# GpSimd shares in unpacking the first two weights and forms w_in's sums, with a new order of work up to the first products

## The chip, the cores and the metric

The kernel runs on one core of a Trainium2 chip. Its engines work side by side, each through its own list of instructions in order, and wait for each other by semaphores: TensorE (PE in the profile, its weight loads PEld), VectorE (DVE), ScalarE (ACT), GpSimd (POOL) and SyncE (SP), which issues the transfers. The metric is the device time of one execution in microseconds; lower is better.

## The reference

Attention within chunks of 64 rows, then two MLPs on 2304 tokens of width 512:

```python
q_c = q.reshape(B, H, nc, 64, D)            # B 4, H 8, 9 chunks, D 64; k, v alike
scores = scale * np.matmul(q_c, k_c.transpose(0, 1, 2, 4, 3))
attn = softmax(scores)                      # max taken off, sum + 1e-9
x = heads_side_by_side(np.matmul(attn, v_c))        # 2304 x 512
h = x @ w_in                                # 512 x 2048
g = np.maximum(h, 0.0) + alpha * np.minimum(h, 0.0)
x = g @ w_out                               # 2048 x 512
out = ((x @ w_a) * (x @ w_b)) @ w_out2      # 512 x 1536 twice, 1536 x 512
```

The weights come in as 64-bit floats; the kernel reads each as two 32-bit words and unpacks them itself.

## The kernel before

A float32 product is made of three matmuls on rounded parts: every operand is split into a high part `hi` (a rounded copy, made by ACT in `to_hi`, L88) and a low part `lo` (the rest, made by DVE in `to_lo`, L93), and `three` (L390) multiplies high by high, high by low and low by high.

A weight passes through three stages. `w_load` (L113) brings a raw tile of 128 x 1024 words in by a transfer on SP. `unpack_ops` (L127) makes 512 floats per row of it: one step widens the upper word by a scale of 2^-112 into the tile `wx`; two 16-bit steps form `wz`, its lower half from the lower word's upper bits and its upper half from the sign bit; a last DVE step (L159) shifts `wx` left by three and puts `wz` in. With `act_first` 2, ACT does the widening (L140) and the lower half of `wz` (L145), DVE the sign (L156) and the combining. Then `w_parts` takes the result and `to_hi` and `to_lo` split it. The units of weights are, in order, i0, i1, i2, o0, i3, o1, i4, o2 and so on, where i is a tile of w_in and o one of w_out; raw tiles 0, 1, 2 lie in three staging buffers that later loads reuse.

The tokens go in blocks of 512, 256, 512, 512 and 512. The first block's attention is four units of 128 tokens, written out by hand in one string, `order1` (L1198): each word is a letter and a number, and the string is the order in which instructions enter the engines' lists. F n: n filler transposes on PE. k, q: transposes of k and q. S: scores. M: maximum and subtraction. X: exponential. N: one step of four of the softmax's division. P: transpose of the probabilities. O: product with v. H, L: high and low part of the attention result x. U i: one step of three of unpacking weight i. C, D: high and low part of a weight (ACT, DVE). A2, A4: the first projection (weight i0) over the first and the second 256 tokens of the block. B, G: the activation's parts. After the string the loop over 16 tiles j of w_in runs (L1310): `s1` projects with i j, `s2` accumulates with o j two tiles behind, and `prelu_unpacking` (L433) makes the activation and unpacks two further weights for each j of the first block.

PSUM tiles for the early attention are taken in turn from two pools of four banks (`att_bank`, L289); a bank is free when its last reader is done.

In blocks 1 and 2 `keep_sum` (L167) adds the two parts of each w_in tile up to the whole value again, and `keep_out` (L174) writes it to DRAM (`wd`), 16 tiles, to be read back for blocks 3 and 4. POOL is used for the identity matrix and constants alone.

Of the kernel before, what the change touches and what calls it, by code (L numbers as in the profile page):

```python
# [8 lines left out]
F32 = mybir.dt.float32  # L9
F32R = mybir.dt.float32r  # L10
I32 = mybir.dt.int32
U16 = mybir.dt.uint16
AF = mybir.ActivationFunctionType
ALU = mybir.AluOpType
# [4 lines left out]
def chunk_attention_prelu_mlp_bilinear_mlp(  # L19
# [17 lines left out]
    nc = tc.nc  # L37
# [38 lines left out]
    def bank(nm="ps"):  # L76
        return ps_p.tile([P, DM], F32, tag="ps", name=nm)
# [6 lines left out]
    def wtile(name, dt=F32R):  # L84
        return wp.tile([P, DM], dt, tag="w", name=name)

    def to_hi(hi, lo, src):
        nc.scalar.activation(out=hi, in_=src, func=AF.Copy)  # L88

    def to_lo(hi, lo, src):  # L90
        if lo is None:
            return
        nc.vector.tensor_tensor(out=lo, in0=src, in1=hi.bitcast(F32), op=ALU.subtract)  # L93

    def split(*a):
        to_hi(*a)
        to_lo(*a)
# [13 lines left out]
    W, raws, xs, slots = {}, {}, {}, {}  # L111
# [15 lines left out]
    def unpack_ops(i, act_first=False):  # L127

        raw = raws.pop(i)
        hw = raw.rearrange("p (f t) -> p f t", t=2)[:, :, 1]
        xs[i] = x = wtile("wx", I32)
        z = wtile("wz", I32)
        z2 = z.bitcast(U16).rearrange("p (f t) -> p f t", t=2)
        h2 = raw.bitcast(U16).rearrange("p (f t) -> p f t", t=4)

        def widen():
            return nc.scalar.activation(out=x.bitcast(F32), in_=hw.bitcast(F32), func=AF.Copy, scale=2.0 ** -112)  # L140

        if act_first == 2:

            widen()
            yield nc.scalar.activation(  # L145
                out=z2[:, :, 0], in_=h2[:, :, 1], func=AF.Copy, scale=2.0 ** -13, bias=2.0 ** -14 - 0.5
            )
        else:
            if act_first:
                yield widen()  # L150
            yield nc.vector.tensor_scalar(
                out=z2[:, :, 0], in0=h2[:, :, 1], scalar1=13, scalar2=None, op0=ALU.logical_shift_right
            )
            if not act_first:
                yield widen()
        yield nc.vector.tensor_scalar(  # L156
            out=z2[:, :, 1], in0=h2[:, :, 3], scalar1=1 << 15, scalar2=None, op0=ALU.bitwise_and
        )
        yield nc.vector.scalar_tensor_tensor(  # L159
            out=x, in0=x, scalar=3, in1=z, op0=ALU.logical_shift_left, op1=ALU.bitwise_or  # L160
        )

    wd = [dr.tile([P, DM], F32, name=f"wd{j}") for j in range(J1)]

    whole = []

    def keep_sum(j):  # L167

        hi, lo = W["i", j]
        x = wtile("wi", F32)  # L170
        nc.vector.tensor_tensor(out=x, in0=hi.bitcast(F32), in1=lo.bitcast(F32), op=ALU.add)
        whole.append((j, x))

    def keep_out(n):  # L174
# [209 lines left out]
    def xtiles(nm):  # L384
        return (
            xp.tile([P, KD, NB], F32R, tag="xh", name=nm + "h"),
            xp.tile([P, KD, NB], F32R, tag="xl", name=nm + "l"),
        )

    def three(ps, w, x, i, n_i):  # L390
        (wh, wl), (xh, xl) = w, x
        for a, b, first in ((wh, xh, True), (wh, xl, False), (wl, xh, False)):
            nc.tensor.matmul(  # L393
                out=ps, lhsT=a, rhs=b, start=(i == 0 and first), stop=(i == n_i - 1 and a is wl)
            )

    def proj(w, x, n, ps=None, lo=0):
        ps = ps or bank("psh")
        for kk in range(KD):
            f = slice(kk * P, (kk + 1) * P)  # L400
            three(ps[:, lo:n], (w[0][:, f], w[1][:, f]), (x[0][:, kk, lo:n], x[1][:, kk, lo:n]), kk, KD)
        return ps
# [147 lines left out]
    parts = {}  # L550
# [588 lines left out]
    with tc.manual_schedule():  # L1139
# [13 lines left out]
        x = xtiles("x")  # L1153
# [17 lines left out]
        chains, parts, h0, g0 = {}, {}, [], []  # L1171

        def chained(key, chain, u):
            if (key, u) not in chains:
                chains[key, u] = chain(u)
            next(chains[key, u])
# [11 lines left out]
            "H": lambda u: each(to_hi, parts["x", u]),  # L1188
            "L": lambda u: each(to_lo, parts["x", u]),
            "W": w_dma,  # L1190
            "U": lambda i: chained("U", lambda i: unpack_ops(i, 2), i),
            "B": lambda i: nc.scalar.activation(out=beta_sb, in_=alpha_sb, func=AF.Copy, scale=-1.0, bias=1.0),
            "G": lambda i: chained("G", lambda i: prelu_parts(0, h0[0], g0, True), i),
            "C": lambda i: (parts.update({("w", i): w_parts(i)}), to_hi(*parts["w", i])),
            "D": lambda i: to_lo(*parts["w", i]),
            "A": lambda u: h0.append(proj(W["i", 0], x, u * P, *h0, lo=len(h0) * n0 // 2 * P)),
        }
        order1 = (  # L1198
# [3 lines left out]
        )  # L1202
        for t in order1.split():
            early[t[0]](int(t[1:]))
# [74 lines left out]
        for b, (t0, n) in enumerate(blocks[:bx]):  # L1279
# [66 lines left out]
            x = nxt  # L1346
# [215 lines left out]
        for p, j in seq:  # L1562
# [8 lines left out]
            if not left[j] and j + 2 < J2:  # L1571
# [5 lines left out]
                i = units.index(("b", j + 2)) + 1  # L1577
# [89 lines left out]
```

## Time and profile before

| | |
|---|---|
| time, median of 3 runs | 848.49 us (848.29 to 848.98) |
| span of the profiled execution | 845.1 us |
| PE busy | 833.5 us, 99% |
| DVE busy | 647.7 us, 77% |
| ACT busy | 420.2 us, 50% |
| POOL busy | 0.7 us, 6 instructions |

The span is that of one profiled execution, from its first to its last instruction; that execution's own time outside the profiler isn't given, so the span stands beside the median of the runs. A busy time is a union over instructions, so neighbours that overlap count once; an instruction's duration is longer than the distance to the next start on its engine. What an engine is worth is read from the stretch: which wait ends last there.

### The profile page before, as it was taken

How to read it: one execution, taken by the hardware profiler on the slowest of the kernel's cores; microseconds unless marked ns; L12 is line 12 of the kernel's file. 1: busy time of each engine (PE TensorE's matmuls, PEld its weight loads, DVE VectorE, ACT ScalarE, POOL GpSimd, SP SyncE). 2: the span in 40 equal slices, each digit the busy share in tenths (PEclk: the TensorE clock that was granted, in tenths of full speed). 3: DMA queues.
4: the chain of work that ended last, by engine and by line, in shares of the span. 5: the costliest groups of instructions: out<-in, count | busy, mean ns of one | idle time of the engine just before them, and what ended most of it. 6: DMA issues, size and time to landing. Idle time of an engine off the chain costs nothing.

```text
span 845.1 us, 14464 instructions
## 1 busy us (share of the span) xinstructions
PE 833.5 (99%) x5429; PEld 714.1 (84%) x5429; DVE 647.7 (77%) x1236; ACT 420.2 (50%) x794; POOL 0.7 (0%) x6
## 2 busy tenths in 40 slices
PE   7999999999999999999999999999999999999998
PEld 6788889988787788888888888888888888889998
DVE  5899955656778877777969888898898858848781
ACT  5998955566656553445643223323333236533440
POOL 0000000000000000000000000000000000000000
PEclk9999999999999999999999999999999999999999
DMA  9994759989963412053801554544454158825511
GB/s 214 284 287 163 200 130 222 233 206 223 231 181 100 150 50 100 26 188 136 299 26 57 187 170 149 168 177 148 155 206 144 75 198 303 282 64 176 152 60 52
DMA packets 171655, 138.86 MB, mean 164 GB/s; under 512 B 101825, under 2 KB 138177, under 8 KB 171585
## 3 DMA queue, kind: packets, MB, share of 16 engines
q1 hardware_dynamic: 171584, 137.93, 55.6%
q8 instruction: 43, 0.70, 0.4%
q14 instruction: 28, 0.22, 0.1%
HBM read 82.32 MB, written 46.40 MB: 152 GB/s over the span
## 4 chain that ended last, share of the span: by engine, by line
PE 90%; DVE 4%; ACT 3%; DMA 2%; issue 1%; SPq 0%; DVEq 0%; ACTq 0%
PE acc L393 27%; PE psh L393 11%; PE psA L615 8%; PE psD L615 8%; PE psB L615 8%; PE psr L393 4%; PE psE L615 4%; PE psD L759 3%; PE psB L759 3%; PE psA L759 3%; PE psD L1365 3%; PE psB L1365 3%; PE psA L1365 2%; PE psE L759 2%; PE psE L1365 1%; PE psSO L315 1%
## 5 line engine op out<-in xcount | busy, mean ns | idle before, releaser
L159 DVE SCALAR_TENSOR_TENSOR wx<-wx,wz 128x512 int32<-128x512 int32 x68 | 46.9, 689 | 14.3 <-ACT wx L140 10.8
L88 ACT ACTIVATE gh<-pos 128x512 fp32r<-128x512 f32 (+1 forms) x56 | 31.8, 567 | 38.8 <-DVE pos L415 32.3
L649 ACT ACTIVATE p<-psA 128x512 f32<-128x512 f32 x24 | 14.4, 598 | 71.7 <-PE psA L615 71.7
L93 DVE TENSOR_TENSOR gl<-pos,gh 128x512 fp32r<-128x512 f32 (+1 forms) x56 | 34.4, 615 | 20.2 <-ACT gh L88 19.1
L645 DVE TENSOR_TENSOR t<-p,psB 128x512 f32<-128x512 f32 x48 | 32.9, 685 | 21.4 <-PE psB L615 17.2
L415 DVE SCALAR_TENSOR_TENSOR pos<-neg,nalpha_sb,pos 128x256 f32<-128x256 f32 (+1 forms) x32 | 19.7, 617 | 28.9 <-ACT pos L413 28.6
L655 ACT ACTIVATE p<-psD 128x512 f32<-128x512 f32 x24 | 14.4, 599 | 50.9 <-PE psD L615 42.4
L411 ACT ACTIVATE neg<-psh 128x512 f32<-128x512 f32 (+1 forms) x48 | 24.7, 515 | 12.6 <-PE psh L393 12.6
L140 ACT ACTIVATE wx<-raw 128x512 f32<-128x512 f32 x48 | 30.2, 661 | 0.0
L683 ACT ACTIVATE b_sb<-psr 128x256 f32<-128x256 f32 x12 | 4.6, 382 | 51.6 <-PE psr L393 51.6
L393 PE MATMUL psr<-xrh,Tl 128*128 128x256 f32 x96 | 27.2, 283 | 0.0
L393 PE MATMUL psr<-xrl,Th 128*128 128x256 f32 x96 | 27.2, 283 | 0.0
L393 PE MATMUL psr<-xrh,Th 128*128 128x256 f32 x96 | 27.1, 282 | 0.0
L1376 DVE SCALAR_TENSOR_TENSOR pos<-neg,beta_sb,psA 128x512 f32<-128x512 f32 x8 | 6.0, 748 | 25.9 <-ACT neg L1372 25.9
L266 ACT ACTIVATE kqd<-kq 128x1024 uint16<-128x1024 uint16 x24 | 24.1, 1046 | 2.6 <-DMA kq<-in_k_dram 2.2
L156 DVE TENSOR_SCALAR wz<-raw 128x512 uint16<-128x512 uint16 x48 | 21.4, 453 | 0.0
L1372 ACT ACTIVATE neg<-p 128x512 f32<-128x512 f32 x24 | 15.2, 633 | 8.8 <-DVE p L1405 8.0
L393 PEld LDWEIGHTS psr<-xrl,Th 128*128 128x128 f32 x96 | 18.4, 192 | 0.4
L393 PEld LDWEIGHTS psr<-xrh,Th 128*128 128x128 f32 x96 | 18.4, 192 | 0.4
L1376 DVE SCALAR_TENSOR_TENSOR p<-neg,beta_sb,p 128x512 f32<-128x512 f32 x24 | 18.0, 749 | 0.8
L393 PEld LDWEIGHTS psr<-xrh,Tl 128*128 128x128 f32 x96 | 18.4, 192 | 0.0
L645 DVE TENSOR_TENSOR p<-t,p 128x512 f32<-128x512 f32 x24 | 16.6, 692 | 1.0
(949 smaller groups left out, 3009.3 us busy)
## 6 DMA issues: line engine op xcount, KB each, us to landing
raw<-in_moe_w_out_dram SPq DMA_DIRECT2D x17, 512.0 KB, 4.1
raw<-in_moe_w_a_dram SPq DMA_DIRECT2D x12, 512.0 KB, 5.1
raw<-in_moe_w_b_dram SPq DMA_DIRECT2D x12, 512.0 KB, 4.9
cd<-t SPq DMA_DIRECT2D x24, 256.0 KB, 2.2
cd<-p SPq DMA_DIRECT2D x24, 256.0 KB, 2.0
room<-in_moe_w_out_dram SPq DMA_DIRECT2D x11, 512.0 KB, 5.4
room<-in_moe_w_in_dram SPq DMA_DIRECT2D x9, 512.0 KB, 5.2
v<-in_v_dram SPq DMA_DIRECT2D x16, 256.0 KB, 4.6
```

The lines of the kernel that those rows point to most:

```text
L88: nc.scalar.activation(out=hi, in_=src, func=AF.Copy)
L93: nc.vector.tensor_tensor(out=lo, in0=src, in1=hi.bitcast(F32), op=ALU.subtract)
L140: return nc.scalar.activation(out=x.bitcast(F32), in_=hw.bitcast(F32), func=AF.Copy, scale=2.0 ** -112)
L159: yield nc.vector.scalar_tensor_tensor(out=x, in0=x, scalar=3, in1=z, op0=ALU.logical_shift_left, op1=ALU.bitwise_or)
L266: nc.scalar.activation(out=d, in_=src.bitcast(U16).rearrange("p (f t) -> p t f", t=2), func=AF.Copy)
L393: nc.tensor.matmul(out=ps, lhsT=a, rhs=b, start=(i == 0 and first), stop=(i == n_i - 1 and a is wl))
L411: up = nc.scalar.activation(out=neg, in_=h, func=AF.Relu, scale=-1.0)
L615: nc.tensor.matmul(out=ps, lhsT=a, rhs=b, start=(start and kk == 0 and i == 0), stop=(kk == 1 and i == 2), skip_group_check=not start,)
L645: nc.vector.tensor_tensor(out=out, in0=a, in1=b, op=op)
L759: nc.tensor.matmul(out=ps[:, s * HALF:(s + 1) * HALF], lhsT=a, rhs=x[:, e], start=(start and s == 0 and i == 0 and n == 0), stop=(i == J2 ...
L1365: nc.tensor.matmul(out=ps, lhsT=a, rhs=b_, start=(start and kk == 0 and i == 0), stop=(kk == 1 and i == 2), skip_group_check=not start,)
L1376: nc.vector.scalar_tensor_tensor(out=out_, in0=neg, scalar=beta_sb[:, j:j + 1], in1=h, op0=ALU.mult, op1=ALU.add)
```

## The change

POOL gets three kinds of work. `unpack_pool` is a second form of unpacking: POOL widens the upper word and forms the sign half (as a comparison with 32768 times 32768), DVE makes the lower half of `wz` by a shift and combines. Weights 0 and 1 go this way, in three steps each (Y). `pool_lo` makes the low part of a weight on POOL (E), for weights 0 and 1 in place of D. `keep_sum` adds on POOL.

`order1` is rewritten from unit 1's scores on. The first half projection A2 now stands ahead of unit 3's transpose P3 and product O3, where it had stood behind them. All of unit 3's softmax division (N3) stands behind weight 0's DVE steps and the low parts of units 0 and 1. Weights 2 and 3 (U2, U3) begin after the second half projection A4 is in PE's list and after x's last high part on ACT. The filler transposes go from 49 to 32.

```diff
+    def pool_lo(hi, lo, src):
+        nc.gpsimd.tensor_tensor(out=lo, in0=src, in1=hi.bitcast(F32), op=ALU.subtract)
...
+    def unpack_pool(i):
+        raw = raws.pop(i)
+        hw = raw.rearrange("p (f t) -> p f t", t=2)[:, :, 1]
+        xs[i] = x = wtile("wx", I32)
+        z = wtile("wz", I32)
+        z2 = z.bitcast(U16).rearrange("p (f t) -> p f t", t=2)
+        h2 = raw.bitcast(U16).rearrange("p (f t) -> p f t", t=4)
+        pool = nc.gpsimd
+        pool.tensor_scalar(
+            out=x.bitcast(F32), in0=hw.bitcast(F32), scalar1=2.0 ** -112, scalar2=None, op0=ALU.mult
+        )
+        yield pool.tensor_scalar(
+            out=z2[:, :, 1], in0=h2[:, :, 3], scalar1=32768.0, scalar2=32768.0, op0=ALU.is_ge, op1=ALU.mult
+        )
+        yield nc.vector.tensor_scalar(
+            out=z2[:, :, 0], in0=h2[:, :, 1], scalar1=13, scalar2=None, op0=ALU.logical_shift_right
+        )
+        yield nc.vector.scalar_tensor_tensor(
+            out=x, in0=x, scalar=3, in1=z, op0=ALU.logical_shift_left, op1=ALU.bitwise_or
+        )
...
-        nc.vector.tensor_tensor(out=x, in0=hi.bitcast(F32), in1=lo.bitcast(F32), op=ALU.add)
+        nc.gpsimd.tensor_tensor(out=x, in0=hi.bitcast(F32), in1=lo.bitcast(F32), op=ALU.add)
...
+            "Y": lambda i: chained("Y", unpack_pool, i),
...
+            "E": lambda i: pool_lo(*parts["w", i]),
...
-            "N2 M3 F6 P1 X3 N2 N2 N2 U0 N3 O0 O1 F9 P2 U0 N3 H0 N3 H1 N3 F5 O2 U1 P3 U0 F5 O3 C0 L0 L1 D0 "
-            "H2 H3 F6 A2 U2 U1 L2 L3 U1 A4 U3 C1 B0 U2 D1 G0 U2 G0 C2 D2 G0 U3 U3 G0 "
+            "Y0 Y1 N2 M3 F6 P1 X3 N2 N2 N2 O0 O1 F4 H0 H1 P2 Y0 Y0 C0 E0 L0 L1 N3 N3 N3 N3 O2 F4 A2 H2 P3 "
+            "Y1 Y1 O3 C1 E1 L2 H3 L3 A4 U2 U3 B0 U2 G0 U2 G0 C2 D2 G0 U3 U3 G0 "
```

## Rows read from the trace of the kernel before

**Rows 1.** The page, part 1: busy us, share of the span, instructions.
```profile
PE 833.5 (99%) x5429; PEld 714.1 (84%) x5429; DVE 647.7 (77%) x1236; ACT 420.2 (50%) x794; POOL 0.7 (0%) x6
```

**Rows 2.** Ten-us stretches: length, busy us (instructions) by engine, granted clock, DMA share, GB/s.
```profile
40.00:50.00 10.00, 10.00 (x50) 8.41 (x49) 9.98 (x18) 10.00 (x19) 0.00 (x0) 1.00 1.08 320
...
160.00:170.00 10.00, 9.46 (x128) 8.79 (x127) 5.94 (x15) 5.87 (x18) 0.00 (x0) 1.00 0.93 231
...
270.00:280.00 10.00, 9.62 (x40) 7.12 (x40) 8.50 (x23) 5.70 (x17) 0.00 (x0) 1.00 0.25 96
```

**Rows 3.** Waits of PE, whole span: who for whom, us, times, longest.
```profile
PE psSO L315 <- DMA qT<-rowsq: 1.1, 2, 0.5
...
PE psSO L369 <- ACT eT L353: 0.5, 1, 0.5
...
PE acc L393 <- ACT gh L88: 0.2, 1, 0.2
```

**Rows 4.** Timeline of DVE and ACT, 14 to 24: start, length, instruction.
```profile
14.43 0.68 DVE L341 TENSOR_REDUCE sm<-e 128x8 f32<-128x512 f32 x1
...
15.58 0.69 DVE L345 TENSOR_TENSOR e<-e,rc 128x512 f32<-128x512 f32 x1
...
18.55 0.69 DVE L345 TENSOR_TENSOR e<-e,rc 128x512 f32<-128x512 f32 x1
...
18.76 0.67 ACT L140 ACTIVATE wx<-raw 128x512 f32<-128x512 f32 x1
...
19.75 0.45 DVE L156 TENSOR_SCALAR wz<-raw 128x512 uint16<-128x512 uint16 x1
...
21.13 0.68 DVE L159 SCALAR_TENSOR_TENSOR wx<-wx,wz 128x512 int32<-128x512 int32 x1
21.73 1.41 DVE L93 TENSOR_TENSOR xl<-psO,xh 128x256 fp32r<-128x256 f32 x4
```

**Rows 5.** Timeline of the chain to the first products, 22 to 38.
```profile
22.54 0.66 PE L351 MATMUL psP<-ident,e 128*128 128x128 f32 x4 [0.89 <-DVE xl L93]
...
23.88 0.69 PE L369 MATMUL psO<-eT,v 64*64 64x64 f32 x32
...
26.79 0.39 PE L393 MATMUL psh<-xl,wi0h 128*128 128x256 f32 x1
...
28.57 0.19 PEld L393 LDWEIGHTS psh<-xh,wi1h 128*128 128x128 f32 x1 [0.42 <-ACT wi1h L88]
...
29.30 0.19 PEld L393 LDWEIGHTS psh<-xh,wi1l 128*128 128x128 f32 x1 [0.43 <-DVE wi1l L93]
...
31.70 0.39 PE L393 MATMUL psh<-xh,wi2h 128*128 128x512 f32 x1
...
37.51 0.19 PEld L393 LDWEIGHTS psh<-xh,wi3l 128*128 128x128 f32 x1 [0.18 <-DVE wi3l L93]
```

**Rows 6.** Instructions of L171, the sums: the first and last of 16.
```profile
L171 DVE TENSOR_TENSOR wi<-wi0h,wi0l x1: 681/681/681, 124.9 to 124.9; 128x512 f32<-128x512 f32 x1
...
L171 DVE TENSOR_TENSOR wi<-wi15h,wi15l x1: 683/683/683, 250.5 to 250.5; 128x512 f32<-128x512 f32 x1
```

**Rows 7.** Timeline of POOL, two of its six instructions.
```profile
0.34 0.10 POOL L1651 MEMSET const-uint8-127<- 128x1 uint8 x1
...
1.01 0.29 POOL masks.py:199 TENSOR_SCALAR_AFFINE_SELECT ident<-ident 128x128 f32<-128x128 f32 x1
```

**Rows 8.** Issues of the first two raw tiles; then their KB and us to landing.
```profile
8.59 1.09 SPq L123 DMA_DIRECT2D raw<-in_moe_w_in_dram  x1
...
11.70 3.58 SPq L123 DMA_DIRECT2D raw<-in_moe_w_in_dram  x1
...
raw<-in_moe_w_in_dram SPq DMA_DIRECT2D x1, 512.0 KB, 6.9
...
raw<-in_moe_w_in_dram SPq DMA_DIRECT2D x1, 512.0 KB, 7.2
```

**Rows 9.** The last stretch of the span, columns as in rows 2.
```profile
843.50:845.10 1.60, 0.00 (x0) 0.00 (x0) 0.00 (x0) 0.00 (x0) 0.00 (x0) 0.64 0.11 36
```

## The prediction

> **What bounds the kernel now.** I read the page first: TensorE (PE) is busy 833.5 of 845.1 us [rows 1]. So only the time in which PE is idle or does no product can be won, and the next view, busy time in ten-microsecond stretches, says where that is. From 30 us on nearly every stretch shows PE at 10.00 of 10.00; the exceptions are five stretches between 160 us, which lacks 0.54, and 280 us, whose last ten lack 0.38, 2.25 us together [rows 2]. Before 30 us PE waits for attention results and weights. So the change can act in two places: on the time at which PE's unbroken run begins, and on those 2.25 us, of which two waits, 1.1 us together, end on a DMA transpose that the change doesn't touch [rows 3].
>
> The third view is the timeline of 15 to 38 us. VectorE (DVE) works without a gap through the softmax of units 1, 2 and 3, unpacks w_in's first tile and splits x [rows 4]. Then one chain runs through PE, ScalarE (ACT) and DVE: the transpose of unit 3's probabilities at 22.54 (held by the PSUM bank that the first x split was reading), its copy on ACT, the product with v at 23.88, the two-part split of x, and the second half of the first projection at 26.79. After that PE waits twice for the second weight tile, until 28.57 for its high part and until 29.30 for its low part, so the third tile's product starts at 31.70. At 37.51 it waits once more, 0.18 us, for wi3's low part [rows 5]. From there PE doesn't stop until after 160 us. Whatever the new order gains must therefore still be there at about 37.5 us; and between 40 and 50 us ACT is busy 10.00 and DVE 9.98 of 10 us [rows 2], so PE can start earlier only if their work comes earlier too.
>
> **The change, step by step.** *Removed.* ACT loses four unpacking instructions for weights 0 and 1; the first took 0.67 us [rows 4], so at least 2.7 us. DVE loses the 16 sums of w_in, 0.68 each [rows 6], 10.9 us, and two low-part subtractions of the same shape, 1.4 us. DVE's two unpacking steps per tile stay two. 17 of 49 filler transposes go; they cost only where PE is late.
>
> *Added on GpSimd (POOL).* Four unpacking instructions, two subtractions, 16 sums. The trace has no POOL instruction of this size. The nearest row is the select over 128x128, 0.29 us, against 0.10 us for a fill of one column [rows 7]. Four times as many elements give 0.10 + 4 x 0.19 = 0.86, or 1.16 us if all of it scales; from below, DVE's 0.45 [rows 4] and 0.68 [rows 6] for the same shapes. I take 0.8 for an unpacking step and 1.1 for a two-input step, nearest to POOL's own row.
>
> *When POOL can begin.* The first raw tile is issued at 8.59 and lands 6.9 us later, 15.5; the second at 11.70 + 7.2 = 18.9 [rows 8]. So POOL does weight 0 from 15.5 to 17.1 and weight 1 from 18.9 to 20.5. The first is wanted at 19.5 by DVE's combining step, the second at 24: both are covered. The subtraction for wi0's low part stands behind weight 1's two steps, since POOL is in order; it can begin when wi0's high part is there, 20.9 below, so it slips from the point where an unpacking step takes over 1.0 us.
>
> *The chain.* Up to the multiply of unit 2's softmax, at 18.55, DVE's list is unchanged. Neighbours overlap a little: the combining step of 0.68, at 21.13, has its successor at 21.73, 0.60 later [rows 4]; I take 0.61 for a 0.69 step and 0.34 for the 0.45 one. So the shift of weight 0 begins at 19.16, combining at 19.50, the four x splits from 20.10 to 21.4, and unit 3's softmax, which in unit 1 took 1.84 from sum to end (14.43 to 16.27, rows 4), ends at 23.3. In the kernel before it had ended when the combining step began, at 21.13 [rows 4], so this moves back by 2.2. But the transpose had stood until 22.54 behind a bank; now the bank's readers are done by 21.4. Transpose, copy and product, which took from 22.54 to 23.88 + 0.69 [rows 5], 2.03, then two ACT pieces and the last DVE piece, about 1.15, end at 26.5. The second half of the projection starts at 26.5, not 26.79: 0.3 us won.
>
> *The wait that goes.* wi0's parts: high on ACT from 20.2 to 20.9 behind copies that take its freed time, low on POOL by 22.0; the first half projection (1.4 us) fits ahead of the transpose at 23.3. wi1's low part is ready by about 26.5. So the two waits on wi1 vanish. The second tile's twelve matmuls took 31.70 - 28.57 - 0.43 = 2.7 us without the wait [rows 5], and the second half's twelve, of half the columns, 1.4. So the third tile begins at 26.5 + 1.4 + 2.7 = 30.6 or 30.7 instead of 31.70: 1.0 us won.
>
> *What is late next.* Units 2 and 3 are now unpacked on ACT after x's split, 2.6 us from 25.9 to 28.5, where they had been done by 28.05, so the activation's first step comes at 28.7 and the following ACT and DVE steps run only about 0.6 us ahead of before. The wait at 37.51 on wi3 catches up with PE. Of the 1.0 us, 0.6 is kept.
>
> *POOL beside DVE.* No row shows both at work, so what they cost each other is bounded: nothing, or a full wait of one for the other. POOL's weight 1 steps, 18.9 to 20.5, lie right on DVE's combining step at 19.50 and the multiply at 18.55; waiting for one of them costs 0.6 (19.50 to 20.1), for both 1.4, and the last multiply behind POOL's subtraction another 0.6: 0 to 2.0 us on the DVE chain, on which everything above hangs. I take 0.3, near the free end, because only one DVE step with two SBUF operands meets POOL.
> The Trainium skill (SBUF — State Buffer, Who interferes with whom) speaks against the change here: a DVE step with two SBUF inputs and a POOL step that reads SBUF exclude each other for a whole instruction. By that rule the combining step waits for at least one POOL step, and the sum would be -0.2 in place of -0.5; no run here shows it yet.
>
> *The 16 sums.* They lie between 124.9 and 251.2 us [rows 6], where DVE is idle for some 40% of a stretch [rows 2], and nobody waited for them but SP's write to DRAM. Their removal frees DVE ahead of the activation's steps; of the 2.25 us the waits that end on ACT or DVE are 0.5 + 0.2 and a few tenths more [rows 3]. I take 0.2 won. Against it stand up to 1.2 us of waiting per sum on a DVE step, which DVE's idle time covers. The writes queue on SP behind POOL's result; POOL has nothing else to do by then, so they come no later. In the start, the reload of the second raw buffer waits on DVE's last read, now some 1 us sooner, and nothing queued on SP comes later.
>
> Sum: -0.6 + 0.3 - 0.2 = -0.5 us. The profiled execution's span is 845.1 us; the median is 848.49, so 3.4 us lie around the span, which no edit touches. 848.49 - 0.5 = 848.0.
>
> **Rivals.** *POOL is slow* (the slower side). If an unpacking step takes 2 us, weight 0 ends at 19.5, weight 1 at 23.5, wi0's low part at 25.5, and the first half projection ends near 27.0. Unit 3's transpose stands behind it in PE's order, so it starts at 27.0 in place of 23.3: 3.7 later, and -0.6 + 3.7 - 0.2 is 2.9 slower than before, 851.4. It decides from 1.0 us a step. For it: two operations in one instruction, on strided 16-bit data, unlike the select. Against it: the select's 0.29. Chance 0.12.
>
> *POOL holds DVE*: a full wait of up to 2.0 us in the start against a gain of 0.8 gives up to +1.2, and further waits in the sums' stretches might add as much again. I put it at 849.2. For: the overlap in time; against: one two-operand step alone meets it. Chance 0.25.
>
> *The start and the sums both pay in full*: 1.0 kept, and all that isn't a DMA wait of the 2.25, 1.15: 848.49 - 2.2 = 846.3. Against it: wi3's wait. Chance 0.09.
>
> *The clock*. PE has fewer fillers, and a gap of about 1 us before the second half projection. The granted clock is 1.00 in each stretch [rows 2] and falls only at the end, to a mean of 0.64 in a stretch in which PE has no work at all [rows 9]. If it fell to its lower level, 1.2 of 2.4 GHz, the second half and the second tile's product, 4.1 us, would take up to 4.1 us more, of which PE's lead hides some: 850 to 852. Chance 0.04.
>
> **How the numbers follow.** The forecast has 0.50 (847.4 to 848.4). Up to 846.8 lies some 0.09, over 850.5 some 0.12; the range 846.7 to 850.5 takes in the bound of the waits and leaves 2 in 10 out. 0.2%, about what a measurement of this kernel can tell from no change, is 1.7 us: faster (under 846.8) 0.10, slower (over 850.2) 0.17, the same 0.73.
>
> **What will show it.** In the profile after: POOL's unpacking steps at 15.5 and 18.9 with about 0.8 us each; the second half projection near 26.5; no wait of PE on wi1; the third tile's product near 30.7; a wait on wi3 of some 0.4 us near 37; the same 2 us of idle PE between 160 and 280 us. Wrong would be POOL steps over 1.0 us, a first half projection that waits for wi0's low part, DVE steps that begin late with nothing named but POOL, or a sum stretch with more PE idle time than before.

## The result and the profile after

The changed kernel takes 855.35 us (median of six runs, 852.08 to 857.06) against 848.39 us for the kernel before (six runs, 846.85 to 848.98): a ratio of 1.0077 [1.0059, 1.0096]. It is 7 us slower. (A ratio in this document is taken over the runs, and is not the quotient of the two medians.) The profiled execution's span is 855.0 us against 845.1. The six runs of the changed kernel fall into two groups by the granted clock: four show a mean granted PE clock of 0.994 to 0.996 and take 855.0 to 857.06 us, the profiled one among them; two show 1.00 and take 852.08 and 852.53.

The page, part 1, of the changed kernel; the line of before is [rows 1].

```profile
PE 837.4 (98%) x5412; PEld 716.1 (84%) x5412; DVE 647.2 (76%) x1218; ACT 418.0 (49%) x790; POOL 32.0 (4%) x28
```

PE is busy 3.9 us longer with 17 instructions fewer, and idle 6.0 us longer (17.6 of 855.0 against 11.6 of 845.1). DVE lost 16 sums, two subtractions and 10.9 + 1.4 us of work by the prediction's count, but its busy time fell by 0.5 us only: the steps that it kept have become longer.

The timeline of the changed kernel's start: start, length, engine and line, instruction, and in brackets the idle time before it and what ended that. Here stand the rows that answer to [rows 4, 5, 8].

```profile
14.01 1.55 POOL L176 TENSOR_SCALAR wx<-raw 128x512 f32<-128x512 f32 x1 [12.72 <-DMA raw<-in_moe_w_in_dram]
...
15.03 0.55 DVE L368 TENSOR_SCALAR sm<-sm 128x8 f32<-128x8 f32 x1
15.54 2.11 POOL L179 TENSOR_SCALAR wz<-raw 128x512 uint16<-128x512 uint16 x1
...
15.86 0.85 DVE L371 TENSOR_TENSOR e<-e,rc 128x512 f32<-128x512 f32 x1
...
19.20 1.88 POOL L176 TENSOR_SCALAR wx<-raw 128x512 f32<-128x512 f32 x1 [1.55 <-DMA raw<-in_moe_w_in_dram]
...
19.59 0.92 DVE L182 TENSOR_SCALAR wz<-raw 128x512 uint16<-128x512 uint16 x1
...
20.62 0.69 DVE L185 SCALAR_TENSOR_TENSOR wx<-wx,wz 128x512 int32<-128x512 int32 x1
21.04 2.28 POOL L179 TENSOR_SCALAR wz<-raw 128x512 uint16<-128x512 uint16 x1
...
23.25 1.26 POOL L96 TENSOR_TENSOR wi0l<-wx,wi0h 128x512 fp32r<-128x512 f32 x1
23.27 1.26 DVE L368 TENSOR_SCALAR sm<-sm 128x8 f32<-128x8 f32 x1
...
24.57 0.39 PE L419 MATMUL psh<-xh,wi0l 128*128 128x256 f32 x1 [1.48 <-POOL wi0l L96]
...
24.81 0.69 DVE L371 TENSOR_TENSOR e<-e,rc 128x512 f32<-128x512 f32 x1
...
25.86 1.05 PE L377 MATMUL psP<-ident,e 128*128 128x128 f32 x4
...
29.48 0.58 PE L419 MATMUL psh<-xh,wi0h 128*128 128x256 f32 x1 [0.74 <-ACT xh L88]
...
32.51 0.48 PE L419 MATMUL psh<-xh,wi1h 128*128 128x512 f32 x1
...
35.34 0.39 PE L419 MATMUL psh<-xh,wi2h 128*128 128x512 f32 x1
```

Read it from the top. POOL's unpacking steps take 1.55 to 2.28 us, its subtraction 1.26. Two DVE steps over 128x8 elements, 0.55 and 1.26 us, lie beside POOL instructions; the second begins and ends with POOL's subtraction. DVE's combining step at 20.62 lies beside POOL's widening (19.20 to 21.08) and the comparison behind it, and takes 0.69, as in [rows 4] (0.68). PE waits 1.48 us for weight 0's low part. Unit 3's division ends at 24.81 + 0.69 = 25.50, but its transpose starts at 25.86, when PE has done the rest of the first half projection, at which it had been without a gap since 24.57: what came last here is the low part from POOL, not the division from DVE. The second half projection starts at 29.48 and the third tile's product at 35.34, 3.64 us later than in [rows 5]. The two waits of [rows 5] on wi1 are gone, as the change intends, and nothing is won by it.

Stretches of the changed kernel: length, busy us (instructions) of PE, PEld, DVE, ACT and POOL, granted clock, DMA share, GB/s, as in [rows 2].

```profile
22.00:25.00 3.00, 1.30 (x9) 0.91 (x8) 2.90 (x6) 0.53 (x2) 2.51 (x2) 1.00 0.54 97
25.00:28.00 3.00, 2.31 (x29) 1.91 (x30) 2.23 (x5) 1.05 (x2) 0.00 (x0) 0.64 1.06 347
28.00:31.00 3.00, 2.26 (x33) 1.84 (x28) 1.43 (x4) 2.30 (x6) 1.26 (x1) 0.50 0.96 317
...
226.00:228.00 2.00, 1.36 (x57) 1.39 (x61) 0.45 (x1) 0.00 (x0) 0.00 (x0) 0.81 0.94 236
228.00:230.00 2.00, 2.00 (x23) 1.59 (x16) 0.00 (x0) 1.60 (x4) 1.28 (x1) 0.50 1.96 196
...
140.00:290.00 150.00, 144.31 (x1375) 120.66 (x1374) 100.39 (x229) 88.87 (x193) 18.33 (x14) 0.99 0.81 189
```

PE was busy 1.30 of the 3 us from 22 to 25; then its granted clock was 0.64, and 0.50 (1.2 of 2.4 GHz) from 28 to 31. The second half projection's twelve matmuls took 32.51 - 29.48 = 3.03 us, against the 1.4 of the prediction. The clock fell a second time at 226. The last row is the stretch of the sums. The same row of the kernel before:

```profile
140.00:290.00 150.00, 147.76 (x1366) 123.78 (x1357) 107.67 (x253) 91.98 (x198) 0.00 (x0) 1.00 0.80 190
```

PE's idle time there went from 2.24 to 5.69 us. One place shows how; the timeline of the changed kernel at 224:

```profile
224.64 1.26 POOL L197 TENSOR_TENSOR wi<-wi13h,wi13l 128x512 f32<-128x512 f32 x1 [7.38 <-PE psh L419]
...
225.04 1.41 DVE L371 TENSOR_TENSOR e<-e,rc 128x512 f32<-128x512 f32 x1
...
226.64 0.94 PE L341 MATMUL psSO<-kT,qT 64*64 64x64 f32 x30 [1.92 <-DVE e L371]
```

The softmax multiply, 0.69 us in [rows 4], starts 0.40 after a POOL sum, takes 1.41 us, and PE waits 1.92 us for it. Its clock is 0.81 and then 0.50 in the rows above.

So the time went to three places: the start (third tile +3.64 us, the clock's fall in it), the sums' stretch (PE idle +3.45 us), and matmuls at the lower clock there. The last block-2 use of weight o0 starts at 297.7 instead of 288.1, 9.6 later, and the span is 9.9 longer.

### The profile page after: what moved, and what is told of

It is laid out like the page before. It is cut to its first block, busy times and chain, and to the rows that moved or that the text cites. A ratio compares the mean times of both kernels' runs of the same rounds, so it can differ in the third digit from the quotient of the medians.

```text
span 855.0 us, 14469 instructions
## 1 busy us (share of the span) xinstructions
PE 837.4 (98%) x5412; PEld 716.1 (84%) x5412; DVE 647.2 (76%) x1218; ACT 418.0 (49%) x790; POOL 32.0 (4%) x28
## 4 chain that ended last, share of the span: by engine, by line
PE 84%; DVE 4%; DMA 4%; ACT 4%; SPq 2%; issue 1%; POOL 1%; DVEq 0%; ACTq 0%
PE acc L419 24%; PE psh L419 10%; PE psA L641 8%; PE psD L641 7%; PE psB L641 7%; PE psE L641 4%; PE psr L419 3%; PE psB L785 3%; PE psD L785 3%; PE psA L785 3%; PE psB L1393 3%; PE psD L1393 3%; PE psA L1393 2%; PE psE L785 2%; PE psE L1393 1%
## 5 line engine op out<-in xcount | busy, mean ns | idle before, releaser
L93 DVE TENSOR_TENSOR gl<-pos,gh 128x512 fp32r<-128x512 f32 (+1 forms) x56 | 37.9, 678 | 20.2 <-ACT gh L88 19.6
L441 DVE SCALAR_TENSOR_TENSOR pos<-neg,nalpha_sb,pos 128x256 f32<-128x256 f32 (+1 forms) x32 | 22.0, 689 | 37.5 <-ACT pos L439 37.3
```

## The experiments

Theory A: POOL and DVE hold each other, instruction by instruction; POOL's long steps make both the start and the sums' stretch late. Rival B: the new order by itself is the loss, whatever engine does the work. Rival C: PE's clock is the loss, because the new order leaves it gaps. In each set the kernel before ran beside the experiments; its median was 847.63, 847.66 and 847.74 us in the three sets, and every ratio below is to the kernel before in its set.

### The sums: sums_dve, sums_pool, sums_quarters

The changed kernel with the sums back on DVE:

```diff
-        nc.gpsimd.tensor_tensor(out=x, in0=hi.bitcast(F32), in1=lo.bitcast(F32), op=ALU.add)
+        nc.vector.tensor_tensor(out=x, in0=hi.bitcast(F32), in1=lo.bitcast(F32), op=ALU.add)
```

> The changed kernel with the 16 sums of w_in back on DVE; the start as changed. Theory (the start and the sums each cost of their own): the third tile's product still begins near 35.3 as in the changed kernel (31.70 before), but PE's idle time between 140 and 290 us falls from about 5.7 us back to 2 to 2.5, so the median is 850.5 to 852.5. Rival (the stalls between 140 and 290 us come from the later start, which shifts everything against the transfers, and not from the sums): the idle time stays and the median stays at 854 to 856.

Measured: 850.28 us, 1.0037 [1.0023, 1.0052]. Stretch of the sums of this kernel, columns as above:

```profile
140.00:290.00 150.00, 146.94 (x1402) 123.75 (x1402) 105.78 (x252) 91.40 (x199) 0.00 (x0) 1.00 0.85 198
```

PE is idle 3.06 us there instead of 5.69, where 2 to 2.5 had been expected, and the start is no earlier than in the whole change (third tile at 36.47). Of the 7.0 us, 2.7 remain (850.28 - 847.63), a little under the range that had been expected. How that splits between sums and start is not clean, since the runs differ by the clock here too: seven at 0.997 to 1.00 take 848.25 to 851.13 us, three at 0.994 take 852.43 to 854.35; that is three of ten at the lower clock, where the whole change had four of six.

The reverse, the kernel before with only its sums moved to POOL:

```diff
-        nc.vector.tensor_tensor(out=x, in0=hi.bitcast(F32), in1=lo.bitcast(F32), op=ALU.add)
+        nc.gpsimd.tensor_tensor(out=x, in0=hi.bitcast(F32), in1=lo.bitcast(F32), op=ALU.add)
```

> The kernel before with the 16 sums alone moved to POOL. Theory: the start is as before (third tile near 31.7), DVE's steps beside a sum take up to 1.3 us more, and PE's idle time between 120 and 290 us rises by 3 us or more: 851 to 854. Rival (POOL beside DVE costs nothing that PE sees, as the prediction had it): 848 to 848.6, with DVE's steps at their old lengths.

Measured: 849.87 us, 1.0027 [1.0018, 1.0036], +2.2 us: between the two expectations, above the rival's 848.6 and short of the theory's 851. The stretch, and a part of its timeline:

```profile
140.00:290.00 150.00, 145.58 (x1340) 121.27 (x1333) 103.92 (x234) 89.70 (x194) 19.12 (x14) 1.00 0.82 189
```
```profile
151.82 1.30 POOL L171 TENSOR_TENSOR wi<-wi4h,wi4l 128x512 f32<-128x512 f32 x1 [9.10 <-DMA wd<-wi]
...
152.41 0.98 DVE L93 TENSOR_TENSOR gl<-pos,gh 128x256 fp32r<-128x256 f32 x1 [0.48 <-ACT gh L88]
...
153.06 1.48 POOL L171 TENSOR_TENSOR wi<-wi5h,wi5l 128x512 f32<-128x512 f32 x1
...
153.32 1.50 DVE L415 SCALAR_TENSOR_TENSOR pos<-neg,nalpha_sb,pos 128x256 f32<-128x256 f32 x1
...
155.31 0.43 DVE L93 TENSOR_TENSOR gl<-pos,gh 128x256 fp32r<-128x256 f32 x1 [0.48 <-ACT gh L88]
```

The activation's low part takes 0.98 us beside a sum and 0.43 beside none; the activation's last step 1.50. PE, which wants both, is idle 4.42 us in the stretch, 2.2 more than before: the whole of the +2.2. The start is the old one, so this is the sums' cost alone, at full clock.

If one POOL instruction holds one DVE step for its length, then shorter POOL instructions should hold it less, though they are more work in all. The kernel before, each sum on POOL in four pieces:

```diff
-        nc.vector.tensor_tensor(out=x, in0=hi.bitcast(F32), in1=lo.bitcast(F32), op=ALU.add)
+        for c in range(0, DM, P):
+            s_ = slice(c, c + P)
+            nc.gpsimd.tensor_tensor(
+                out=x[:, s_], in0=hi[:, s_].bitcast(F32), in1=lo[:, s_].bitcast(F32), op=ALU.add
+            )
```

> The kernel before with the 16 sums on POOL, each in four pieces of 128 columns; all else as before. Theory (a DVE step that meets a sum waits for the end of one POOL instruction): a wait is at most some 0.35 us instead of 1.3, PE's idle time between 140 and 290 us goes back from 4.4 towards 2.2 to 3, and the time is 847.9 to 849. Rival (DVE loses by POOL's total work on SBUF, not by the length of one instruction): 849.5 to 850.5 as with whole sums.

Measured: 847.54 us, 0.9996 [0.9987, 1.0006], a little better than expected. Its stretch of the sums, columns as above:

```profile
140.00:290.00 150.00, 147.89 (x1361) 123.70 (x1354) 102.17 (x238) 92.77 (x198) 28.24 (x56) 1.00 0.81 190
```

POOL is busy 28.24 us instead of 19.12, and PE is idle 2.11 us, as in the kernel before. What costs is the length of one POOL sum at the moment when DVE's step is due, not POOL's work in total. Whether the freed DVE gives the prediction's 0.2 us then can't be told from nothing.

### The clock: clock_fill, start_fill

The changed kernel with more filler transposes for PE at the three places where it had gaps:

```diff
-N3 N3 N3 N3 O2 F4 A2 H2 P3 Y1 Y1 O3 C1 E1 L2 H3 L3 A4
+N3 N3 N3 N3 O2 F22 A2 H2 P3 F10 Y1 Y1 O3 C1 E1 L2 H3 L3 F9 A4
```

> The changed kernel with 37 more filler transposes in the places where PE sat idle between 21.7 and 29.5 us, so that PE's clock has no reason to fall. Theory (the fall of the clock to 0.50 between 25 and 33 us is paid in full: the second half projection took 3.0 us instead of 1.4): granted clock 1.00 throughout, the third tile 2 to 2.5 us earlier than 35.3, median 851.5 to 853.5. Rival (the engines behind PE set the start, so a slower PE costs nothing): the clock stays up but the median is 854.5 or more.

Measured: 852.67 us (851.19 to 853.49), 1.0055 [1.004, 1.007]. The stretches that were at 0.64 and 0.50 in the changed kernel:

```profile
25.00:28.00 3.00, 3.00 (x55) 2.83 (x53) 1.49 (x4) 1.12 (x2) 0.31 (x1) 1.00 1.01 366
28.00:31.00 3.00, 2.99 (x35) 2.73 (x27) 1.82 (x4) 2.79 (x6) 0.97 (x1) 1.00 1.03 369
```

With PE busy the clock stays at 1.00, and the third tile starts at 33.60 instead of 35.34. The time is near that of the two runs of the changed kernel at clock 1.00 (852.08, 852.53). So the clock's fall goes with the 3.6 us between those two and the median of the other four, 855.94 (of the six, only one of these four has a trace); at full clock most of the loss remains, 5.0 us here (852.67 - 847.63) and 3.9 in those two runs (852.3 - 848.4). Rival C explains a part, not the whole.

The same with the sums on DVE, that is the changed start alone at full clock (the edits of clock_fill and sums_dve together):

> The whole new start with the fillers that keep the clock up, and the sums on DVE: what POOL and the order cost in the start without the clock and without the sums. Theory (start, clock and sums each have a price of their own): third tile near 33.6, granted clock 1.00, no DVE step between 110 and 280 us stretched, 849.2 to 850.2, which is 0.2 to 0.3% over the kernel before. Rival (the start's loss is mostly the clock's): 847.6 to 848.6.

Measured: 849.81 us, 1.0025 [1.0016, 1.0034], third tile at 33.83. The start costs 2.1 us with the clock held up. Against clock_fill the sums cost 2.9 us here, against 2.2 alone.

### The parts of the start: order_only, order_fill, unpack_pool, low_dve

The new order with the old engines, no work on POOL:

```diff
-N2 N2 N2 U0 N3 O0 O1 F9 P2 U0 N3 H0 N3 H1 N3 F5 O2 U1 P3 U0 F5 O3 C0 L0 L1 D0 H2 H3 F6 A2 U2 U1 L2 L3 U1 A4 U3 C1 B0 U2 D1 ...
+N2 N2 N2 U0 O0 O1 F4 H0 H1 P2 U0 U0 C0 L0 L1 D0 N3 N3 N3 N3 O2 F4 U1 A2 H2 P3 U1 U1 O3 C1 D1 L2 H3 L3 A4 U2 U3 B0 U2 ...
```

> The kernel before with the new order of the start, but the old engines: ACT and DVE unpack weights 0 and 1 and DVE makes their low parts; ACT's steps stand where its list has room. Theory (POOL's long steps and DVE's waiting for them make the start slow, the order by itself does not): the second half projection starts at 26.5 to 27.5 and the third tile at 30.7 to 31.9, the granted clock stays 1.00, 847.5 to 849. Rival (the order is what costs: unit 3's division has moved behind the splits): the third tile after 33 and 850 or more.

Measured: 851.05 us, 1.0034 [1.0024, 1.0045]: theory A's number was missed, and B's time came. Two things are mixed in it: the granted clock is 0.71 from 20 to 25, and wi1's low part (D1), which stands ahead of x's last split in DVE's list, waited 1.73 us for ACT and made that split late. So the next kernel has fillers and D1 behind the split:

```diff
-O0 O1 F4 H0 H1 ... N3 N3 N3 N3 O2 F4 U1 A2 H2 P3 U1 U1 O3 C1 D1 L2 H3 L3 A4
+O0 O1 F14 H0 H1 ... N3 N3 N3 N3 O2 F6 U1 A2 H2 P3 F10 U1 U1 O3 C1 L2 H3 L3 D1 F9 A4
```

> The new order of the start once more with the old engines, now with the low part of weight 1 behind x's last low part on DVE and with fillers in PE's gaps, so that neither a DVE step that waits for ACT nor the clock disturbs it. Theory (in the run before of this kind the third tile's 33.83 came from that DVE step and from the clock, which was down to 0.71 between 20 and 25 us): granted clock 1.00, third tile at 31.2 to 32.2, 847.5 to 849. Rival (the order itself costs, because unit 3's division has moved back and ACT can't finish its copies in time): third tile at 33 or later, 850 or more.

Measured: 848.89 us, 1.0017 [1.0008, 1.0026], clock 1.00. From its timeline:

```profile
24.82 0.63 PE L351 MATMUL psP<-ident,e 128*128 128x128 f32 x4 [0.18 <-DVE e L345]
```

The order alone, with full clock and no POOL, still costs 1.2 us and starts the third tile at 32.58, 0.9 us later than [rows 5]; 31.2 to 32.2 had been expected. Unit 3's transpose waits for unit 3's division on DVE and starts at 24.82, where the prediction had 23.3 for the whole change. With the division behind weight 0's steps, all that delays those steps delays it too: DVE's combining waits 0.54 us for ACT here, and wi0's low part, 0.69, stands ahead of the division. These two are what POOL takes over in the change, so B holds for a part, 1.2 us, with the old engines (its own 850 us and third tile after 33 didn't come), and this kernel is no clean price of the order under POOL.

The other part alone, the old order with POOL's two unpacking steps for weights 0 and 1, low parts and sums on DVE:

```diff
-N2 M3 F6 P1 X3 N2 N2 N2 U0 N3 O0 O1 F9 P2 U0 N3 H0 N3 H1 N3 F5 O2 U1 P3 U0 F5 O3 ... A2 U2 U1 L2 L3 U1 A4
+Y0 Y1 N2 M3 F6 P1 X3 N2 N2 N2 N3 O0 O1 F9 P2 Y0 N3 H0 N3 H1 N3 F5 O2 P3 Y0 F5 O3 ... A2 U2 Y1 L2 L3 Y1 A4
```

> One part of the change alone: POOL takes its two steps of unpacking weights 0 and 1; the order, the low parts and the sums as before. Theory (POOL's 1.5 to 2.3 us steps hold DVE's softmax back wherever both want SBUF): DVE's steps between 15 and 24 us stretch by 1 to 2.5 us together, and the second half projection starts 0.5 to 2 us after 26.8: 848 to 850. Rival (ACT's 2.9 us of freed time outweighs it): the third tile starts earlier than 31.7, below 847.6.

Measured: 848.14 us, 1.0005 [0.9996, 1.0014]. From its timeline:

```profile
21.67 1.15 DVE L185 SCALAR_TENSOR_TENSOR wx<-wx,wz 128x512 int32<-128x512 int32 x1
...
23.54 0.66 PE L377 MATMUL psP<-ident,e 128*128 128x128 f32 x4 [1.36 <-DVE xl L93]
```

DVE's combining step is 1.15 us long instead of 0.68 [rows 4], and the bank wait of [rows 5] grows from 0.89 to 1.36. The third tile starts at 32.53, 0.8 us late, so the rival's earlier start did not come. The time lies at the low end of the expected 848 to 850; its interval reaches to +1.2 us and takes the 0.8 in, but doesn't tell it from nothing.

Last, start_fill with the low parts back on DVE:

```diff
-C0 E0 L0 L1 N3 ... O3 C1 E1 L2 H3 L3 F9 A4
+C0 L0 L1 D0 N3 ... O3 C1 L2 H3 L3 D1 F9 A4
```

> The same, with the low parts of weights 0 and 1 back on DVE, behind x's splits; POOL only unpacks. Theory (DVE is held so long by POOL's unpacking steps that unit 3's division, not wi0's low part, comes last ahead of unit 3's transpose): wi0's low part comes earlier than in the changed kernel (24.5), the division later by up to 0.7, the time 849.2 to 850.5. Rival (wi0's low part, queued in POOL behind weight 1's steps, sets the pace): about 1 us less than the run with the low parts on POOL, 848.2 to 849.

Measured: 849.52 us, 1.0021 [1.0011, 1.003], third tile at 34.01: no difference to start_fill that the intervals can tell. The two don't separate the low parts well, because the fillers set the start of the first half projection in both (24.58 and 24.75): in start_fill wi0's low part was ready 0.6 us earlier than that. What the low parts on POOL cost in the changed kernel is therefore read from its timeline alone, the 1.48 us wait at 24.57 and the addition over 128x8 that took 1.26.

### The price of POOL's steps and who is held: bench, bench2

Behind the kernel before stands a tail of POOL and DVE steps; only the steps' lengths are read. In the first, POOL has three of each form alone, then DVE's forms run alone and beside twelve sums.

```diff
+        for _ in range(3):
+            G.tensor_scalar(out=px, in0=bhw.bitcast(F32), scalar1=2.0 ** -112, scalar2=None, op0=ALU.mult)
+        for _ in range(3):
+            G.tensor_scalar(out=px, in0=be, scalar1=2.0, scalar2=None, op0=ALU.mult)
...
+        dve()
...
+        for _ in range(12):
+            G.tensor_tensor(out=px, in0=be, in1=bf, op=ALU.add)
+        dve()
```

> The kernel before with a tail of measurements: POOL's steps alone (widening from every second word, the same from dense words, the 16-bit comparison, a sum of two tiles), three of each; DVE's steps alone (reduction, 128x8 addition, sum of two SBUF tiles, sum of one PSUM and one SBUF tile, 16-bit shift, combining), two of each; then the same DVE steps beside a row of POOL sums. Its time means nothing. Theory (DVE and POOL exclude each other for a whole instruction when DVE needs its second SBUF path): alone, widening takes 1.5, the comparison 2.1, the sum 1.26; beside POOL, the sum of two SBUF tiles and the combining take up to 1.26 us more, the reduction and the sum with PSUM keep their times; whether the 128x8 addition and the shift are held is what I want to see. Rival (both only share bandwidth): all DVE steps and POOL's stretch by a similar share.

The timeline of the tail, POOL alone:

```profile
847.22 4.70 POOL L1661 TENSOR_SCALAR px<-braw 128x512 f32<-128x512 f32 x3 [845.94 <-DMA braw<-in_moe_w_in_dram]
852.01 4.63 POOL L1663 TENSOR_SCALAR px<-be 128x512 f32<-128x512 f32 x3
856.60 6.42 POOL L1665 TENSOR_SCALAR pz<-braw 128x512 uint16<-128x512 uint16 x3
862.96 3.94 POOL L1667 TENSOR_TENSOR px<-be,bf 128x512 f32<-128x512 f32 x3
```

One widening takes 1.57 us from every second word and 1.54 from dense words, one comparison 2.14, one sum 1.31. Reading every second word is not the reason for the long widening. Beside POOL's sums DVE's combining took 1.60 us instead of 0.69, the 128x8 addition 0.52 instead of 0.17, the 16-bit shift 0.80 instead of 0.45; the reduction, and a sum with one operand in PSUM, took the same. A sum of two SBUF tiles took 0.68, not longer, where more had been expected; that it stood right behind a step that had been held may be why, but isn't shown. Two of each form are few, so the second tail has five of each form, alone and beside 20 of each POOL form:

```diff
+        for other in beside:          # nothing, widening, comparison, sum
+            if other is not None:
+                for _ in range(20):
+                    other()
+            for form in forms:
+                for _ in range(5):
+                    form()
```

> The kernel before with a tail of measurements, its time without meaning: six forms of DVE step, five of each, first alone, then beside a row of 20 POOL widenings, then of 20 comparisons, then of 20 sums. Theory (DVE waits for the running POOL instruction's end in every form that uses its second SBUF path): reduction and sum with PSUM keep 0.68 and 0.69, the sum of two SBUF tiles and the combining rise beside each of the three POOL steps, most beside the longest; the 128x8 addition and the 16-bit shift rise too, as beside the sums. Rival (only POOL's two-input sums hold DVE): nothing rises beside widening and comparison.

From its timeline: five of each DVE form alone, then two forms beside POOL's widening, two beside its comparison, and five beside its sums.

```profile
847.72 1.00 DVE L1666 TENSOR_SCALAR bsm<-bsm 128x8 f32<-128x8 f32 x5
848.62 3.59 DVE L1667 TENSOR_TENSOR bd<-ba,bb 128x512 f32<-128x512 f32 x5
852.34 3.59 DVE L1668 TENSOR_TENSOR bd<-bps,bb 128x512 f32<-128x512 f32 x5
855.85 2.40 DVE L1669 TENSOR_SCALAR bz<-braw 128x512 uint16<-128x512 uint16 x5
858.29 3.60 DVE L1672 SCALAR_TENSOR_TENSOR by<-by,bz 128x512 int32<-128x512 int32 x5
...
867.23 4.66 DVE L1667 TENSOR_TENSOR bd<-ba,bb 128x512 f32<-128x512 f32 x5
...
875.43 3.75 DVE L1669 TENSOR_SCALAR bz<-braw 128x512 uint16<-128x512 uint16 x5
...
903.11 3.90 DVE L1667 TENSOR_TENSOR bd<-ba,bb 128x512 f32<-128x512 f32 x5
...
914.47 3.91 DVE L1672 SCALAR_TENSOR_TENSOR by<-by,bz 128x512 int32<-128x512 int32 x5
...
949.12 3.13 DVE L1666 TENSOR_SCALAR bsm<-bsm 128x8 f32<-128x8 f32 x5
952.16 7.35 DVE L1667 TENSOR_TENSOR bd<-ba,bb 128x512 f32<-128x512 f32 x5
959.54 3.59 DVE L1668 TENSOR_TENSOR bd<-bps,bb 128x512 f32<-128x512 f32 x5
963.06 6.20 DVE L1669 TENSOR_SCALAR bz<-braw 128x512 uint16<-128x512 uint16 x5
969.29 8.27 DVE L1672 SCALAR_TENSOR_TENSOR by<-by,bz 128x512 int32<-128x512 int32 x5
```

Beside POOL's sums a DVE step over two SBUF tiles takes twice as long (7.35 for 3.59), the shift 2.6 times (6.20 for 2.40) and the addition over 128x8 three times (3.13 for 1.00); the sum with an operand in PSUM isn't touched. Beside POOL's widening the two-tile sum and the shift lose less (4.66 and 3.75), and beside the comparison, POOL's longest step at 2.14 us, two-tile steps lose least (3.90 for 3.59, 3.91 for 3.60). "Most beside the longest" had been expected, so this expectation failed. Theory A's mechanism is borne out for POOL's two-input steps, the sums. For the unpacking steps the runs contradict it as it stands: DVE is slowed beside them, but doesn't wait for the end of the one that is running.

### A start that keeps the idea: new_start

If the order is at fault and POOL too, then the useful part, wi1 ready in time, should be had from DVE's own idle time. The kernel before with weight 1's DVE steps in the gap ahead of wi0's low part, weight 1's high part right behind x's high parts on ACT, units 2 and 3 later:

```diff
-O3 C0 L0 L1 D0 H2 H3 F6 A2 U2 U1 L2 L3 U1 A4 U3 C1 B0 U2 D1 G0 U2 G0 C2 D2 G0 U3 U3 G0
+O3 C0 L0 L1 U1 U1 D0 H2 H3 F6 A2 C1 U2 L2 L3 D1 A4 U3 U2 U2 B0 U3 U3 G0 G0 C2 D2 G0 G0
```

> The kernel before with DVE's two steps of weight 1 moved into the gap of 1.2 us in which DVE had waited for wi0's high part, weight 1's split right behind x's, and weight 3's DVE steps ahead of the activation's. No POOL work. Theory (the waits on wi1 and wi3 are a matter of order on ACT and DVE): no wait of PE on wi1, third tile at 30.6 to 30.9, 0.6 to 1.0 us of 847.6 less, 846.6 to 847.2. Rival (the sooner start is given back at wi3 or between 140 and 290 us): 847.6 to 848.

Measured: 846.66 us (845.65 to 847.8), 0.9989 [0.998, 0.9998]; it is faster than the changed kernel and, by an interval that only just leaves out no change, than the kernel before. From its timeline:

```profile
28.06 0.40 PE L393 MATMUL psh<-xh,wi1h 128*128 128x512 f32 x1
...
30.81 0.39 PE L393 MATMUL psh<-xh,wi2h 128*128 128x512 f32 x1
```

Weight 1's two DVE steps start at 23.04 and 23.60, the second tile's product without a wait at 28.06, and the third at 30.81 instead of 31.70 [rows 5]. Of these 0.9 us nothing measurable is lost later: 847.66 - 846.66 = 1.0, with 0.2 to 1.7 by the interval. PE doesn't wait for weight 3 either, whose DVE steps had been moved forward too.

## Why the prediction was wrong, step by step

The prediction was 848.0, with a range of 846.7 to 850.5; measured are 855.35. Three terms of its sum failed: POOL's price, POOL beside DVE, and the sums. The clock, which it kept out of the sum, failed too. The order's gain is left in doubt.

**What bounds the kernel** held: every loss sits in PE's wait or clock ahead of 35 us and between 140 and 290 us, the two places named. **What lies around the span** is 857.06 - 855.0 = 2.1 us in the profiled execution. The 3.4 used had set the median against another execution's span; as it stood on both sides, it cost the forecast nothing.

**POOL's price** was the first wrong term. Scaling the 128x128 select [rows 7] gave at most 1.16 us, and 0.8 was taken; measured are 1.57 and 2.14 us alone. A select isn't a price for a widening or a comparison, and the upper bound worked out from it was none. For the two-input step 1.1 was taken, and 1.26 to 1.31 came. The rival "POOL is slow" was right in kind: it wanted steps over 1.0 us and put wi0's low part at 25.5 and unit 3's transpose at 27.0; they came at 24.51 (23.25 + 1.26) and 25.86. Its 851.4 fell short, since it had neither the clock nor the sums.

**When POOL can begin** held nearly: 14.0 and 19.2 for the two raw tiles, against 15.5 and 18.9. **The wait on wi1** vanished, as said. But the wait for wi0's low part, 1.48 us, took its place, by the slip that the prediction had named: POOL is in order, and weight 1's steps stand ahead. wi0's high part had been ready at 21.98, and POOL came to the subtraction at 23.25, behind the comparison of weight 1. This is the step of the prediction that set the start of the profiled execution: of the 4.7 us between the third tile's 35.34 and the predicted 30.6, 2.6 stand at unit 3's transpose (25.86 for 23.3), which the late low part held; the other 2.1 come behind it, in stretches whose granted clock was below 1.00.

**POOL beside DVE** was taken at 0.3 us of 0 to 2.0, on the ground that only one DVE step of two SBUF operands meets POOL. By the prediction's own times unit 1's multiply at 15.58 [rows 4] met POOL too, as did unit 2's at 18.55. Four steps were held in the changed kernel: the addition at 15.03 by 0.38 us, the multiply by 0.16, the shift at 19.59 by 0.47, and the addition at 23.27 by 1.09 (lengths here less those that the same forms have alone). Together 2.1 us, the upper bound and a little more: unit 3's division ended at 25.50 instead of 23.3. In this execution wi0's low part held the transpose longer than that, until 25.86; but with the low part in time, the transpose could still not have started before 25.50. By the rule of the Trainium skill that the prediction weighed (SBUF — State Buffer, Who interferes with whom) a DVE step with two SBUF operands and a POOL step that reads SBUF exclude each other. The trace agrees beside POOL's sums (1.41 us at 225.04 for 0.69; 7.35 for 3.59 in bench2), but not beside its unpacking steps: the combining step at 20.62, which the prediction by that rule let wait for one, took 0.69 beside them (the widening there took 1.88 for 1.57 alone, so POOL may be what lost), and bench2's two-tile sums lost 0.06 to 0.21 us each, far less than a POOL step. A small addition and a 16-bit shift, steps of one tile, were held as well.

**The chain's order** was put 0.3 us ahead of before. order_fill shows the order with the old engines 0.9 us behind, at full clock and with no POOL in it, and start_fill the order with POOL's steps 2.1 behind. No kernel had this order with steps that hold nobody, so that the 0.3 is wrong for such a one isn't shown. The gain that the prediction booked, 1.0 us at the third tile, can be had: new_start has 0.9. There it comes from weight 1's earlier unpacking, without this order. **What is late next**, 0.4 us of waiting on wi3, didn't come in the changed kernel, whose third tile was 3.6 us later than before.

**The clock** had 0.04, on the ground that it had been 1.00 in every stretch [rows 2]. It fell in four of the six runs, and 3.6 us go with that; the one of them that has a trace shows it behind a PE that waited for POOL and DVE. The rival's price, up to 4.1 us, was near in size, partly by luck: of what it named, the second half projection took 1.6 us more (3.03 for 1.4) but the second tile 0.1 (2.83 for 2.7), and a second fall came at 226, which it didn't have. Its chance was too low: the prediction counted the gap of an on-time chain, about 1 us, and each late step above makes that gap longer.

**The sums** were put at -0.2 us because DVE's idle time would cover the steps that are held. They cost 2.2 us alone and 2.9 in the changed kernel at full clock. DVE's idle time is no cover: a step of the activation or of the softmax starts when its input comes, PE is waiting for it, and a POOL sum that runs at that moment delays it (by 0.72 us at 225.04, the 1.41 less 0.69). Idle DVE time in a stretch says that the engine has room, not that its steps may be late.

Added up at full clock: 2.1 for the start (start_fill) and 2.2 (sums_pool) to 2.9 (clock_fill less start_fill) for the sums make 4.3 to 5.0, against the 3.9 of the changed kernel's two runs at clock 1.00. With the clock's 3.6 that is 7.9 to 8.6, against 7.5 in its other four (855.94 - 848.39). So the three terms account for the loss and overshoot it by 0.4 to 1.1 us, which stays unassigned; the fillers, which themselves delay the first half projection, are one reason why it may. How much of the 2.1 is the order and how much POOL in it isn't settled: the order with the old engines costs 1.2, POOL's unpacking in the old order 0.5 and not to be told from nothing, and the low parts couldn't be separated.

## What to carry to other kernels

Work moved to an idle engine isn't free where its instructions hold up another engine's: ask which step of the old engine is due while the new one is in a long instruction, and who waits for that step; cut the moved work into short pieces first, and see whether anything is won at all. Price an operation by the same operation, in a tail of a few steps on the chip, and not by another one scaled up. And where PE's lead is thin, count what a late chain does to PE's clock as a part of the price.

## What the runs showed of the hardware that was not expected

POOL's step with one float input, 1.54 us for 128x512, is slower than its sum of two, 1.31, and a source of every second word costs no more than a dense one (1.57).

What holds DVE goes by form: beside POOL's sums five steps take 3.13 instead of 1.00 us (128x8 addition), 6.20 instead of 2.40 (16-bit shift), 7.35 instead of 3.59 (two SBUF tiles), and 3.59 in both cases with an operand in PSUM. Beside POOL's widening, which is longer than a sum, the sum of two SBUF tiles and the shift lose less, 0.21 and 0.27 us a step (4.66 - 3.59 and 3.75 - 2.40, by five), and beside the comparison, the longest, the sum of two tiles loses 0.06 (3.90 - 3.59, by five); why, stays open. In unpack_pool some DVE steps beside POOL's widening were not held at all, but POOL's spans are rough, so this settles nothing.

PE's granted clock came down to 0.50, 1.2 GHz, behind a stretch in which PE had been busy 1.30 of 3 us, and again behind one wait of 1.92 us in the middle of the kernel; with fillers in the first place it stayed at 1.00.
